# Tables built in place, outer products that ride, and wider VectorE operations in a fused S4D and channel-MLP kernel

## The chip, the cores and the metric

The kernel runs on one core of a Trainium2 chip. The metric is the time of one execution on the device in microseconds. Three runs of the kernel before gave a median of 1099.91 us (1099.19 to 1100.07). The engines are named as in the profile: PE (matrix multiplications), PEld (its weight loads), ACT (functions), DVE (vector operations), POOL and SP (here mostly queues that issue transfers).

## The reference

All arithmetic is in fp32. L is 2048 tokens, D 576 channels, N 128 states a channel, F 4608 hidden units. Cut to what matters:

```python
xn = layernorm(u)                                   # [L, D]
# S4D: a long convolution along the tokens, one kernel a channel
dt = exp(log_dt); A = -exp(log_A_real) + 1j * A_imag; C = (C_real + 1j * C_imag) * dt[:, None]
P = exp((A * dt[:, None])[:, :, None] * arange(L))  # [D, N, L]
K = 2 * einsum("dn,dnl->dl", C, P).real
s = irfft(rfft(xn.T, 2 * L) * rfft(K, 2 * L))[:, :L].T + xn * D_skip
# MLP, gated
y = layernorm(xn)
z = gelu(y @ w1 + b1) @ w2 + b2
out = u + s * silu(z)
```

## The kernel before

**The MLP is the backbone of PE's order.** The hidden units are taken in 12 groups of three times 128 (`NG`, `G`), and the tokens in two halves of two blocks of 512, which makes 48 passes (`slot`). A pass has 11 positions on PE: three layer-1 groups of 14 matmuls of 512 columns (`layer1`, L617), one for each 128 hidden units, and then eight stretches of layer 2 (`layer2`, L680, 288 columns), 72 matmuls. Each fp32 product is split into a high and a low part in fp32r, and three of the four partial products are taken. So for each layer-1 group ACT does the gelu into `h` (L653) and the high part `hh` (L656), and DVE the low part `hl` (L659). Layer 2 starts with the matmuls that need only the first two of the three hidden parts and then comes to the third. DVE adds layer 2's PSUM results to `acc` (L690). Weights come in by DMA into `raw` and are split in the same way (`split_raw`, L570 on ACT and L567 on DVE). In the 23rd and 24th pass the first half's output goes through a tanh for the gate (`gate_store`, L695), and y of the second half is turned and split (`y_turn`).

**The S4D part fills the gaps.** The length-2048 kernel of a channel is an outer product of two tables of powers, summed over the 128 states. `tables(b)` makes them for 16 channels (`SB`; 36 blocks): on DVE `phase` (L914, L917: the angle, 65 places a channel), on ACT `whole` (L920: the whole number of turns), on DVE `frac` (L923), on ACT `fold` (L926) and the two sines `sin` (L931 and L933), on DVE the magnitudes `mags` (L939) and `weigh` (L950 to L956), which multiplies the sines by the magnitudes into the tables `U` (32 places) and `v` (64 places). `kgen(b)` does the outer product on PE (`mm`, L995, 32 matmuls with 32 columns of weights and 64 of data) and copies it out of PSUM on ACT (`out`, L1000, into `kt`). `chunk(c)` then does the transforms of 96 channels (6 chunks): `x1` and `k1` (first stage of the transform for the data and the kernel, with a wide transpose on DVE behind it, L1107 and L1138), `s2` (second stage, L1160, then a copy `kk` on ACT, the products `pr` on DVE, L1175, and their sums, L1181 and L1182), `inverse` (L1202), `back` and `i1` (L1228). `in_parts` makes the high and low parts that `x1` and `k1` read.

**The order is written by a planner in the kernel itself.** The class `Order` holds lines of steps (`tl`, `sl`, `vl`: tables; `kl`: outer products; `c1` to `c4`: chunks) with durations for each engine, conditions (`need`, marks such as `("kg", b)` or `("wu", b, 1)`) and due times (`by`), and pins the resulting order on each engine. `pe_turns` lets S4D work onto PE between positions. An outer product that is ready when `x1`, `k1`, `s2` or `i1` goes can ride in front of it in the same PSUM tile (`ride`, `lead`); otherwise it goes alone when it has waited for `ALONE` us, or 3 us when the next table's sines are done and its due time (`DUE`) has passed. For a step of ACT that needs a table of functions, the planner adds 1.28 for each load; a step that needs none is only tested against the next due time:

```python
                    if st["tbl"]:
                        d += 1.28 * (1 + (st["tbl"] != self.tbl))
                    if b > horizon or b + d > soon.get(e, 1e9) + st["late"]:
                        continue
```

Of the kernel before, what the change touches and what calls it, by code (L numbers as in the profile page):

```python
# [210 lines left out]
def mixer_kernel(ctx, tc, u, log_a_real, a_imag, c_real, c_imag, log_dt, d_skip, w1, b1, w2, b2,  # L211
# [37 lines left out]

    idp = sb.tile([P, P], F32, name="idp")  # L250
    f1t = sb.tile([P, 2, 2, 64], F32, name="f1t")
# [110 lines left out]
    PT0 = 3 * D  # L362

    def table_memory():

        t = [sb.tile([P, 2, SB, NV], F32, name="w", bufs=2) for _ in range(2)]
        t = [x.rearrange("p k c t -> p (k c t)") for x in t + [sb.tile([P, 2, SB, 64], F32, name="v")]]
        return [t[k // 3][:, k % 3 * D:(k % 3 + 1) * D] for k in range(8)]

# [417 lines left out]
    def params():  # L787
# [7 lines left out]
        flat = lambda t: t.rearrange("p a b -> p (a b)")  # L795
        dt = sb.tile([P, 2, SB, 32], F32, name="U").rearrange("p a b c -> p (a b c)")[:, :D]
        PRM = [flat(sb.tile([P, 12, 64], F32, name="kt", bufs=2)) for _ in range(2)]
# [107 lines left out]
    def tables(b):  # L905
# [35 lines left out]

        def weigh(k, part):

            if k == 0 and part == 0:
                T["v"] = sb.tile([P, 2, SB, 64], F32, name="v")
                T["U"] = sb.tile([P, 2, SB, 32], F32, name="U")
                TAB[b] = (T["U"], T["v"])
            w, v, m = T["w"], T["v"], T["m"]
            if part == 0:
                nc.vector.tensor_mul(T["U"][:, k], w[:, k, :, 33:], m[:, :, 64:])  # L950
# [31 lines left out]
    def kgen(b):  # L982
# [16 lines left out]
        def out():  # L999
            nc.scalar.activation(KT[c, r // 48][:, k0:k0 + SB // 4, :].rearrange("p (h i) m -> p h (i m)", h=2),  # L1000
                                 Q[0], AF.Copy)
        need = [("kp", c - 1, r // 48)] if r % 48 == 0 and c else []
        return [step("PE", KG + 0.2, mm, need=need + [("wu", b, 1)], cv=1, mark=("kg", b)),
                step("ACT", act(256), out, cv=-1, mark=("kt", b))]
# [22 lines left out]
    def chunk(c):  # L1027
# [41 lines left out]
        def in_parts(which, i, get, m, need):  # L1069

            def high():
                a = sb.tile([P, 2, 4 * CH], F32R, name="pr").rearrange("p t c -> p (t c)")
                b = sb.tile([P, 2, 4 * CH], F32R, name="ys", bufs=2).rearrange("p t c -> p (t c)")
                PARTS2[which, i] = [t.rearrange("p (c b) -> p c b", b=m) for t in (a, b)]
                nc.scalar.activation(PARTS2[which, i][0], get(), AF.Copy)

            def low():
                a, b = PARTS2[which, i]
                nc.vector.tensor_sub(b, get(), a.bitcast(F32))

            n = 768 if which == "k" else 2000
            four.append(step("ACT", act(n), high, need=need))
            four.append(step("DVE", dve(n), low, mark=(which + "p", c, i)))
# [25 lines left out]

        def k1(i):  # L1110
# [6 lines left out]
            four.append(step("DVE", 0.2, skip, need=kt + ([] if c else [("pack", D // PK - 1), ("f2s", 7), "odd"] if i == 0 else [])))  # L1117
            in_parts("k", i, lambda: KT[c, i], 64, [("k1", c, i - 1) if i else ("x1", c, CH // 48 - 1)])

# [16 lines left out]
            add("PE", X1, mm, cv=2, mark=("k1", c, i), need=[("kp", c, i)] + ([("i1", c - 1)] if c and i == 0 else []))  # L1136
            for g in range(4):
                add("DVE", 0.65, lambda g=g: nc.vector.transpose(  # L1138
                    A2[:, :, 1, 48 * i + 12 * g:48 * i + 12 * g + 12].rearrange("p k d r -> p d k r"),
                    Q[g // 2 * 2][:, g % 2]),  # L1140
                    cv=-(g % 2))

        def s2(p):
# [5 lines left out]
            def mm():  # L1149
# [5 lines left out]
                for i in range(2):  # L1155
                    for ri in range(2):
                        for q in range(4):
                            for f in range(2):
                                r = slice(64 * f, 64 * f + 64)
                                nc.tensor.matmul(Q[i][32 * q:32 * q + 32, f, 2 * ri:2 * ri + 2],  # L1160
                                                 m[r, 4 * i + q, 32 * ri:32 * ri + 32],
                                                 A2[r, 4 * p + 2 * i + q // 2, :, :, q % 2], start=True, stop=True,
                                                 skip_group_check=True)
# [3 lines left out]
            def copy(i):  # L1167
                KK[i] = sb.tile([P, 2, 2, CH], F32, name="kk")
                nc.scalar.activation(KK[i], Q[i][:, :, 1::2], AF.Copy)

            def prod(i):

                PR[i] = sb.tile([P, 2, 4 * CH], F32, name="pr").rearrange("p t (a b d) -> p t a b d", a=2, b=2)
                for t in range(2):
                    nc.vector.tensor_mul(PR[i][:, t], bc(Q[i][:, t, 0::2], 2, 2), bc(KK[i][:, t], 1, 2))  # L1175

            def sums(i):
                if i == 0:
                    Y.append(ys_tile())
                x, y = PR[i], Y[0]  # L1180
                nc.vector.tensor_sub(y[:, i, 0], x[:, :, 0, 0], x[:, :, 1, 1])  # L1181
                nc.vector.tensor_add(y[:, i, 1], x[:, :, 0, 1], x[:, :, 1, 0])  # L1182
            for i in range(2):
                two.append(step("ACT", act(4 * CH), lambda i=i: copy(i), need=[("s2", c, p)]))
                two.append(step("DVE", 0.95, lambda i=i: prod(i), cv=-1))
                two.append(step("DVE", 0.63, lambda i=i: sums(i), mark=("sum", c, p) if i else None))
            if p % 2:
# [547 lines left out]
```

## Time and profile before

| | before |
|---|---|
| median of 3 runs | 1099.91 us (1099.19 to 1100.07) |
| the profiled execution | 1101.59 us |
| its span, first to last instruction | 1099.8 us |
| granted clock of PE | 0.999 |
| busy, PE and DVE and ACT | 1089.1, 918.8, 698.0 us |
| matmuls recorded | 11445 |
| instructions on DVE, on ACT | 1514, 1044 |
| loads of a function table on ACT | 84 |

The page of the profile gives the busy time of each engine, then the span in 40 slices, the DMA queues, the chain that ended last, and the costliest groups of instructions: the line in the kernel, engine, operation, the tiles written and read, the shapes, the count, busy us in all, mean ns of one, and the idle time before them with what ended it. A timeline row has the start in us from the span's start, the length in us, engine, line, tiles, shape and count; matmuls that follow each other in one group are merged into a row, and the recorded ends of matmuls overlap the next one's start, so distances are read from start to start. The same holds for DVE and ACT, whose operations overlap by some 0.1 us when they follow each other without a wait. An fp32 matmul is recorded twice, so the 32 of an outer product stand as 64.

### The profile page before, as it was taken

What the parts mean: (1) busy time and instruction counts of PE and PEld (TensorE: products, weight loads), DVE (VectorE), ACT (ScalarE), POOL (GpSimd) and SP (SyncE); (2) the same over time, 40 slices, a digit from 0 to 9 for tenths busy, and PEclk for the clock granted to TensorE, in tenths of its full rate; (3) what the DMA queues carried; (4) which work ended last, traced back from release to release, by engine and by line L of the source; (5) the groups of instructions that cost most, each with busy time, mean ns of one, the idle gap of its engine ahead of it and who ended that gap; (6) DMA issues with size and microseconds to landing.
All of it is one profiled execution on the core that took longest, in us unless ns stands there. A gap on an engine that the chain in (4) does not pass through costs nothing.

```text
span 1099.8 us, 27208 instructions
## 1 busy us (share of the span) xinstructions
PE 1089.1 (99%) x11445; PEld 953.2 (87%) x11445; DVE 918.8 (84%) x1514; ACT 698.0 (63%) x1044; POOL 184.0 (17%) x255
## 2 busy tenths in 40 slices
PE   8999999999999999999999999999999999999997
PEld 7889989889888888888898888888888888888897
DVE  7698678979998899999999998898998986766356
ACT  6485699867667675676865857566775754324233
POOL 4557211161110100001100000000100012110220
PEclk9999999999999999999999999999999999999999
DMA  8836656735434252355623315242333426453453
GB/s 222 242 131 169 219 173 197 215 71 130 152 115 152 53 112 57 100 128 149 154 51 95 96 56 126 39 143 59 94 89 78 145 66 178 117 178 107 128 148 94
DMA packets 139651, 138.23 MB, mean 126 GB/s; under 512 B 88952, under 2 KB 105016, under 8 KB 138952
## 3 DMA queue, kind: packets, MB, share of 16 engines
q1 hardware_dynamic: 124664, 85.49, 29.6%
q0 software_dynamic: 14384, 50.27, 14.8%
q8 instruction: 89, 1.46, 0.6%
q10 hardware_dynamic: 480, 0.74, 0.3%
q14 instruction: 34, 0.28, 0.1%
HBM read 102.17 MB, written 36.63 MB: 126 GB/s over the span
## 4 chain that ended last, share of the span: by engine, by line
PE 95%; DMA 2%; SPq 2%; DVE 1%; issue 0%; ACTq 0%; ACT 0%; DVEq 0%
PE mxb L680 21%; PE mxa L680 21%; PE mxa L617 20%; PE mxb L617 20%; PE cv L995 3%; PE cv L1160 3%; PE cv L1202 2%; PE cv L1228 2%; PE cv L1130 1%; PE cv L1099 1%; SPq L808 1%; DMA w<-in_A_u_dram 1%; DMA acc<-in_A_u_dram 0%; DVE st L407 0%; DMA h<-in_B_b_dram 0%
## 5 line engine op out<-in xcount | busy, mean ns | idle before, releaser
L659 DVE TENSOR_TENSOR hl<-h,hh 128x512 fp32r<-128x512 f32 x144 | 98.8, 689 | 89.0 <-ACT hh L656 88.3
L680 PE MATMUL mxb<-w2h,hl 128*128 128x288 f32 x576 | 170.2, 295 | 1.8 <-DVE hl L659 1.8
L680 PE MATMUL mxb<-w2h,hh 128*128 128x288 f32 x576 | 171.6, 298 | 0.0
L680 PE MATMUL mxa<-w2h,hh 128*128 128x288 f32 x573 | 170.8, 298 | 0.0
L680 PE MATMUL mxb<-w2l,hh 128*128 128x288 f32 x576 | 169.5, 294 | 0.0
L680 PE MATMUL mxa<-w2h,hl 128*128 128x288 f32 x573 | 169.2, 295 | 0.0
L680 PE MATMUL mxa<-w2l,hh 128*128 128x288 f32 x573 | 168.6, 294 | 0.0
L653 ACT ACTIVATE h<-mxa,b1t 128x512 f32<-128x512 f32 x73 | 50.2, 689 | 110.9 <-PE mxa L617 109.9
L680 PEld LDWEIGHTS mxa<-w2h,hh 128*128 128x128 f32 x573 | 107.6, 188 | 6.6 <-issue 3.5
L680 PEld LDWEIGHTS mxb<-w2h,hh 128*128 128x128 f32 x576 | 108.1, 188 | 5.7 <-issue 1.8
L680 PEld LDWEIGHTS mxb<-w2h,hl 128*128 128x128 f32 x576 | 108.1, 188 | 2.3 <-DVE hl L659 2.3
L680 PEld LDWEIGHTS mxb<-w2l,hh 128*128 128x128 f32 x576 | 108.1, 188 | 0.6
L680 PEld LDWEIGHTS mxa<-w2l,hh 128*128 128x128 f32 x573 | 107.6, 188 | 0.7
L680 PEld LDWEIGHTS mxa<-w2h,hl 128*128 128x128 f32 x573 | 107.5, 188 | 0.1
L896 POOL DMA_DIRECT2D par<-par_s x36 | 27.8, 773 | 462.9 <-DVE mg L939 458.4
L656 ACT ACTIVATE hh<-h 128x512 fp32r<-128x512 f32 x144 | 90.6, 630 | 3.6
L653 ACT ACTIVATE h<-mxb,b1t 128x512 f32<-128x512 f32 x71 | 48.9, 689 | 68.8 <-PE mxb L617 66.4
L690 DVE TENSOR_TENSOR acc<-mxa,acc 128x576 f32<-128x576 f32 x87 | 65.5, 752 | 31.2 <-PE mxa L680 30.9
L617 PE MATMUL mxa<-XH,w1h 128*128 128x512 f32 x284 | 79.1, 400 | 0.0
L690 DVE TENSOR_TENSOR acc<-mxb,acc 128x576 f32<-128x576 f32 x88 | 66.1, 752 | 15.2 <-PE mxb L680 14.8
L617 PE MATMUL mxb<-XH,w1h 128*128 128x512 f32 x280 | 77.7, 399 | 0.0
L617 PE MATMUL mxa<-XL,w1h 128*128 128x512 f32 x284 | 76.1, 390 | 0.0
(269 smaller groups left out, 2483.8 us busy)
## 6 DMA issues: line engine op xcount, KB each, us to landing
raw<-in_B_w_dram SPq DMA_DIRECT2D x72, 288.0 KB, 3.4
raw<-in_B_w_dram SPq DMA_DIRECT2D x96, 192.0 KB, 3.8
par_s<-A POOLq DMA_DIRECT2D x4, 2160.0 KB, 8.2
par<-par_s POOLq DMA_DIRECT2D x36, 240.0 KB, 3.4
f2t<-f2q SPq DMA_DIRECT2D x24, 256.0 KB, 3.4
g2t<-g2p SPq DMA_DIRECT2D x24, 256.0 KB, 4.1
bias<-XR SPq DMA_DIRECT2D x42, 128.0 KB, 3.7
raw<-in_B_w_dram SPq DMA_DIRECT2D x48, 96.0 KB, 3.9
```

Of the source, the lines that this page charges most:

```text
L617: nc.tensor.matmul(q, a, b, start=j == 0 and i not in BEGUN, stop=j == len(ops) - 1, skip_group_check=True)
L653: nc.scalar.activation(t, q, AF.Gelu_apprx_tanh, bias=b1t[:, k:k + 1], scale=1.0)
L656: LAST[0] = nc.scalar.activation(hh[:, i], t, AF.Copy)
L659: nc.vector.tensor_sub(hl[:, i], t, hh[:, i].bitcast(F32))
L680: nc.tensor.matmul(q[:, dh, :288], a[:, i, c], b[:, i, d], start=i == 0 and k == 0 and not alone, stop=i == G - 1 and k == 2)
L690: nc.vector.tensor_add(o, q[:, dh:dh + n, :288], b)
L808: nc.sync.dma_start(r[32 * g:32 * g + 32].rearrange("c (b n) -> c b n", n=32), dram(src[k], 32 * g, [[N, 32], [32 * N, D // 32], [1, 32]]))
L896: nc.gpsimd.dma_start(PAR[b].rearrange("p (g i) k -> p g (i k)", g=4), dram(par_s, (b // 3 * 48 + b % 3 * 4) * NPAR, [[D * NPAR, P], [12 * ...
L995: nc.tensor.matmul(q[32 * g:32 * g + 32, i // 2, i % 2 * 64:i % 2 * 64 + 64], U[:, ri, 4 * g + i, :], v[:, ri, 4 * g + i, :], start=ri == ...
L1160: nc.tensor.matmul(Q[i][32 * q:32 * q + 32, f, 2 * ri:2 * ri + 2], m[r, 4 * i + q, 32 * ri:32 * ri + 32], A2[r, 4 * p + 2 * i + q // 2, :, ...
L1202: nc.tensor.matmul(QI[q // 2][64 * f:64 * f + 64, q % 2, i], MAT["g2t", p + i // 2][r, i % 2, f, ri], YS[p + i // 2][0][r, i % 2, ri, f], ...
L1228: nc.tensor.matmul(Q[h][64 * y:64 * y + 64, t], g1t.rearrange("p a e -> p (a e)"), A2[:, k:k + 2, 1].rearrange("p i d r -> p i r d"), star ...
```

## The change

- The tables are built in place. One tile `w` of 97 places a channel (two of them in turn) holds the 65 angles and, in front, 32 places for the mirrored part. `weigh` has four steps rather than six: two over both sines at once (1024 elements), two of 512. They need the second sine; they no longer wait for `kg` of b-1. In exchange the first step of a table, `phase(0)`, waits for `("kg", b - 2)`, the outer product that read the tile, rather than for `("wu", b - 2, 1)`.
- An outer product goes alone early only when the next table is complete (`wu`, not only its sines), and otherwise after 20 us rather than 12. With `x1` it now rides behind the matmuls instead of in front.
- x's high and low parts are made from a contiguous copy `xt`, which ACT makes in a step of its own (`turn`).
- The transposes behind `x1` and `k1` take 768 elements rather than 384. In `s2` the results are interleaved (`ri::2`), `kk` gets a third, negated part by a second copy on ACT, and with it the products are one operation of 768 rather than two of 384, and the sums one of 384 rather than two of 192.
- The identity lies in the buffer of `f2t`, log dt in one of `ys`, and the early rows of x in two `w` tiles.

The diff, cut to its core:

```diff
-    idp = sb.tile([P, P], F32, name="idp")
+    idp = sb.tile([P, 4, P], F32, name="f2t")[:, 0]
...
+    def table_tile():
+        return sb.tile([P, 2, SB, 32 + NV], F32, name="w", bufs=2)
...
         def phase(k):
             if k == 0:
-                T["w"] = sb.tile([P, 2, SB, NV], F32, name="w", bufs=2)
+                T["v"] = table_tile()
+                T["w"] = T["v"][:, :, :, 32:]
...
+            if part == 0:
+                TAB[b] = (T["w"][:, :, :, 33:], T["v"][:, :, :, :64])
             w, v, m = T["w"], T["v"], T["m"]
             if part == 0:
-                nc.vector.tensor_mul(T["U"][:, k], w[:, k, :, 33:], m[:, :, 64:])
+                nc.vector.tensor_mul(v[:, :, :, :32], w[:, :, :, 32:0:-1], bc(m[:, :, :32], 1, 2))
             elif part == 1:
-                nc.vector.tensor_mul(v[:, k, :, :32], w[:, k, :, 32:0:-1], m[:, :, :32])
-            elif k == 0:
-                nc.vector.tensor_mul(v[:, k, :, 32:], w[:, k, :, :32], m[:, :, 32:64])
+                nc.vector.tensor_mul(w[:, :, :, 33:], w[:, :, :, 33:], bc(m[:, :, 64:], 1, 2))
+            elif part == 2:
+                nc.vector.tensor_mul(w[:, 0, :, :32], w[:, 0, :, :32], m[:, :, 32:64])
             else:
-                nc.vector.scalar_tensor_tensor(v[:, k, :, 32:], w[:, k, :, :32], -1.0, m[:, :, 32:64],
+                nc.vector.scalar_tensor_tensor(w[:, 1, :, :32], w[:, 1, :, :32], -1.0, m[:, :, 32:64],
                                                op0=OP.mult, op1=OP.mult)
...
-                 step("DVE", dve(SB * NV), f(phase, 0), need=[("wu", b - 2, 1)] if b > 1 else []),
+                 step("DVE", dve(SB * NV), f(phase, 0), need=[("kg", b - 2)] if b > 1 else []),
...
-                + [step("DVE", dve(n), f(weigh, k, part), need=[("sin", b, k)] + ([("kg", b - 1)] if b else []),
-                        mark=("wu", b, k) if part == 2 else None) for k in range(2) for part in range(3)])
+                + [step("DVE", dve((2, 2, 1, 1)[part] * n), f(weigh, part), need=[("sin", b, 1)],
+                        mark=("wu", b) if part == 3 else None) for part in range(4)])
...
+            def turn():
+                T["x"] = sb.tile([P, 24, m], F32, name="xt")
+                nc.scalar.activation(T["x"], get(), AF.Copy)
...
+            if which == "x":
+                four.append(step("ACT", act(2000), turn, need=need))
+            four.append(step("ACT", act(768), high, need=need if which == "k" else ()))
+            four.append(step("DVE", dve(768), low, mark=(which + "p", c, i)))
...
-                lead(q)
                 for n, (f, x) in enumerate(((0, a), (0, b), (1, a))):
...
+                lead(q)
             add("PE", X1, mm, cv=2, mark=("x1", c, i), need=[("xp", c, i)])
...
             for d0 in (0, 24):
-                for e in range(2):
-                    c0 = 48 * i + d0 + 12 * e
-                    add("DVE", 0.65, lambda d0=d0, e=e, c0=c0: nc.vector.transpose(
-                        A2[:, :, 0, c0:c0 + 12].rearrange("p k d r -> p d k r"), Q[d0][:, e]), cv=-e)
+                c0 = 48 * i + d0
+                add("DVE", 0.9, lambda d0=d0, c0=c0: nc.vector.transpose(
+                    A2[:, :, 0, c0:c0 + 24].rearrange("p k d r -> p d k r"), Q[d0]), cv=-1)
...
-                                nc.tensor.matmul(Q[i][32 * q:32 * q + 32, f, 2 * ri:2 * ri + 2],
+                                nc.tensor.matmul(Q[i][32 * q:32 * q + 32, f, ri::2],
...
-                KK[i] = sb.tile([P, 2, 2, CH], F32, name="kk")
-                nc.scalar.activation(KK[i], Q[i][:, :, 1::2], AF.Copy)
+                KK[i] = sb.tile([P, 2, 3, CH], F32, name="kk")
+                nc.scalar.activation(KK[i][:, :, :2], Q[i][:, :, :1:-1], AF.Copy)
+                nc.scalar.activation(KK[i][:, :, 2], Q[i][:, :, 3], AF.Copy, scale=-1.0)
...
-                for t in range(2):
-                    nc.vector.tensor_mul(PR[i][:, t], bc(Q[i][:, t, 0::2], 2, 2), bc(KK[i][:, t], 1, 2))
+                x, k = Q[i].rearrange("p t k d -> p t (k d)")[:, :, :2 * CH], KK[i].rearrange("p t k d -> p t (k d)")
+                k = bass.AP(tensor=k.tensor, offset=k.offset + CH, ap=[list(k.ap[0]), list(k.ap[1]), [-CH, 2], [1, 2 * CH]])
+                nc.vector.tensor_mul(PR[i], bc(x, 2, 2), k)
...
-                nc.vector.tensor_sub(y[:, i, 0], x[:, :, 0, 0], x[:, :, 1, 1])
-                nc.vector.tensor_add(y[:, i, 1], x[:, :, 0, 1], x[:, :, 1, 0])
+                nc.vector.tensor_add(y[:, i].rearrange("p a t d -> p t a d"), x[:, :, :, :CH], x[:, :, :, CH:])
...
-    ALONE, DUE = 12.0, (160.0, 950.0)
+    ALONE, DUE = 20.0, (160.0, 950.0)
...
-                    wait = ("sin", b + 1, 1) not in od.marks or od.t["PE"] < DUE[0] + b * (DUE[1] - DUE[0]) / NB
+                    wait = ("wu", b + 1) not in od.marks or od.t["PE"] < DUE[0] + b * (DUE[1] - DUE[0]) / NB
```

More of the change, by code (lines that the diff above doesn't have):

```diff
@@ L362, in mixer_kernel @@
     PT0 = 3 * D
+    def table_tile():
+        return sb.tile([P, 2, SB, 32 + NV], F32, name="w", bufs=2)
     def table_memory():
-        t = [sb.tile([P, 2, SB, NV], F32, name="w", bufs=2) for _ in range(2)]
-        t = [x.rearrange("p k c t -> p (k c t)") for x in t + [sb.tile([P, 2, SB, 64], F32, name="v")]]
-        return [t[k // 3][:, k % 3 * D:(k % 3 + 1) * D] for k in range(8)]
+        t = [table_tile().rearrange("p k c t -> p (k c t)") for _ in range(2)]
+        return [t[k // 4][:, k % 4 * D:(k % 4 + 1) * D] for k in range(8)]
     def x_load(b, queue=nc.sync, two=False):
@@ L795, in params @@
         flat = lambda t: t.rearrange("p a b -> p (a b)")
-        dt = sb.tile([P, 2, SB, 32], F32, name="U").rearrange("p a b c -> p (a b c)")[:, :D]
+        dt = ys_tile().rearrange("p i a b c -> p (i a b c)")[:, :D]
         PRM = [flat(sb.tile([P, 12, 64], F32, name="kt", bufs=2)) for _ in range(2)]
@@ L940, in mags, with weigh @@
                                  bc(PAR[b][:, :, e8:e8 + n], 3, 8), bc(PAR[b][:, :, e1:e1 + 8], 2, n))
[L942 to L947, printed above, removed]
+        def weigh(part):
+            if part == 0:
+                TAB[b] = (T["w"][:, :, :, 33:], T["v"][:, :, :, :64])
             w, v, m = T["w"], T["v"], T["m"]
             if part == 0:
-                nc.vector.tensor_mul(T["U"][:, k], w[:, k, :, 33:], m[:, :, 64:])
+                nc.vector.tensor_mul(v[:, :, :, :32], w[:, :, :, 32:0:-1], bc(m[:, :, :32], 1, 2))
             elif part == 1:
-                nc.vector.tensor_mul(v[:, k, :, :32], w[:, k, :, 32:0:-1], m[:, :, :32])
-            elif k == 0:
-                nc.vector.tensor_mul(v[:, k, :, 32:], w[:, k, :, :32], m[:, :, 32:64])
+                nc.vector.tensor_mul(w[:, :, :, 33:], w[:, :, :, 33:], bc(m[:, :, 64:], 1, 2))
+            elif part == 2:
+                nc.vector.tensor_mul(w[:, 0, :, :32], w[:, 0, :, :32], m[:, :, 32:64])
             else:
-                nc.vector.scalar_tensor_tensor(v[:, k, :, 32:], w[:, k, :, :32], -1.0, m[:, :, 32:64],
+                nc.vector.scalar_tensor_tensor(w[:, 1, :, :32], w[:, 1, :, :32], -1.0, m[:, :, 32:64],
                                                op0=OP.mult, op1=OP.mult)
@@ L1002, in kgen @@
         need = [("kp", c - 1, r // 48)] if r % 48 == 0 and c else []
-        return [step("PE", KG + 0.2, mm, need=need + [("wu", b, 1)], cv=1, mark=("kg", b)),
+        return [step("PE", KG + 0.2, mm, need=need + [("wu", b)], cv=1, mark=("kg", b)),
                 step("ACT", act(256), out, cv=-1, mark=("kt", b))]
@@ L1069, in in_parts, with source @@
         def in_parts(which, i, get, m, need):
+            T = {}
+            def turn():
+                T["x"] = sb.tile([P, 24, m], F32, name="xt")
+                nc.scalar.activation(T["x"], get(), AF.Copy)
+            def source():
+                return get() if which == "k" else T["x"].rearrange("p c b -> p (c b)")
             def high():
[L1072 to L1075, printed above, removed]
+                T["a"] = sb.tile([P, 2, 4 * CH], F32R, name="pr").rearrange("p t c -> p (t c)")
+                T["b"] = sb.tile([P, 2, 4 * CH], F32R, name="ys", bufs=2).rearrange("p t c -> p (t c)")
+                PARTS2[which, i] = [T[k].rearrange("p (c b) -> p c b", b=m) for k in "ab"]
+                nc.scalar.activation(T["a"], source(), AF.Copy)
             def low():
[L1078 to L1083, printed above, removed]
+                nc.vector.tensor_sub(T["b"], source(), T["a"].bitcast(F32))
+            if which == "x":
+                four.append(step("ACT", act(2000), turn, need=need))
+            four.append(step("ACT", act(768), high, need=need if which == "k" else ()))
+            four.append(step("DVE", dve(768), low, mark=(which + "p", c, i)))
         def x1(i):
@@ L1136, in k1 @@
             add("PE", X1, mm, cv=2, mark=("k1", c, i), need=[("kp", c, i)] + ([("i1", c - 1)] if c and i == 0 else []))
[L1137 to L1141, printed above, removed]
+            for g in (0, 2):
+                add("DVE", 0.9, lambda g=g: nc.vector.transpose(
+                    A2[:, :, 1, 48 * i + 12 * g:48 * i + 12 * g + 24].rearrange("p k d r -> p d k r"), Q[g]), cv=-1)
         def s2(p):
@@ L1180, in sums @@
                 x, y = PR[i], Y[0]
-                nc.vector.tensor_sub(y[:, i, 0], x[:, :, 0, 0], x[:, :, 1, 1])
-                nc.vector.tensor_add(y[:, i, 1], x[:, :, 0, 1], x[:, :, 1, 0])
+                nc.vector.tensor_add(y[:, i].rearrange("p a t d -> p t a d"), x[:, :, :, :CH], x[:, :, :, CH:])
             for i in range(2):
-                two.append(step("ACT", act(4 * CH), lambda i=i: copy(i), need=[("s2", c, p)]))
-                two.append(step("DVE", 0.95, lambda i=i: prod(i), cv=-1))
-                two.append(step("DVE", 0.63, lambda i=i: sums(i), mark=("sum", c, p) if i else None))
+                two.append(step("ACT", act(4 * CH) + act(2 * CH), lambda i=i: copy(i), need=[("s2", c, p)]))
+                two.append(step("DVE", dve(8 * CH), lambda i=i: prod(i), cv=-1))
+                two.append(step("DVE", dve(4 * CH), lambda i=i: sums(i), mark=("sum", c, p) if i else None))
             if p % 2:
```

4 lines of the change are left out of this document (2 added, 2 removed).

## The prediction

> **What bounds the kernel now.** I read the page first, then PE's timeline around the groups that the change moves, then ACT's and DVE's timeline where a pass turns from layer 1 to layer 2, and the groups by line and shape last.
>
> ```profile
> PE 1089.1 (99%) x11445; PEld 953.2 (87%) x11445; DVE 918.8 (84%) x1514; ACT 698.0 (63%) x1044; POOL 184.0 (17%) x255
> ...
> PE 95%; DMA 2%; SPq 2%; DVE 1%; issue 0%; ACTq 0%; ACT 0%; DVEq 0%
> ```
>
> PE is busy for 99% of the span and holds 95% of the chain that ended last. So the time is the length of PE's queue plus whatever makes PE wait. DVE at 84% and ACT at 63% are no bound as sums; they count only where PE arrives before their result. Waits of PE look like this in the timeline:
>
> ```profile
> 46.05 0.40 PE L680 MATMUL mxb<-w2h,hl 128*128 128x288 f32 x1 [1.19 <-DVE hl L659]
> 46.28 0.30 PE L680 MATMUL mxb<-w2h,hh 128*128 128x288 f32 x1
> ```
>
> Layer 2 waited 1.19 us for `hl`, and the next matmul came 0.23 after the late one where 0.13 is usual: a wait costs its length and 0.10 for the restart. After the first 50 us I find no further row of this kind: the order fits PE to within its margins. So two questions decide: how much shorter PE's queue gets, and whether the new order makes PE wait.
>
> **PE's queue.** An outer product (`kgen`, 32 matmuls in the program) alone between two layers:
>
> ```profile
> 610.42 0.39 PE L617 MATMUL mxb<-XR,w1s 128*128 128x512 f32 x1
> 610.74 1.10 PE L995 MATMUL cv<-v,U 128*32 128x64 f32 x64
> 611.77 0.96 PE L617 MATMUL mxa<-XH,w1h 128*128 128x512 f32 x3
> ```
>
> One that rides with `s2`, then `s2` without one, then the layer-1 matmuls in front of an `x1` by itself and behind it:
>
> ```profile
> 621.45 0.29 PE L680 MATMUL mxa<-w2h,hl 128*128 128x288 f32 x1
> 621.67 1.10 PE L995 MATMUL cv<-v,U 128*32 128x64 f32 x64
> 622.70 1.62 PE L1160 MATMUL cv<-A,f2t 64*32 64x192 f32 x64
> 624.25 0.40 PE L680 MATMUL mxb<-w2h,hh 128*128 128x288 f32 x1
> 624.49 0.29 PE L680 MATMUL mxb<-w2l,hh 128*128 128x288 f32 x1
> ...
> 632.08 0.39 PE L617 MATMUL mxb<-XR,w1s 128*128 128x512 f32 x1
> 632.39 1.59 PE L1160 MATMUL cv<-A,f2t 64*32 64x192 f32 x64
> 633.91 0.97 PE L617 MATMUL mxa<-XH,w1h 128*128 128x512 f32 x3
> ...
> 679.50 0.39 PE L617 MATMUL mxb<-XR,w1s 128*128 128x512 f32 x1
> ...
> 681.09 0.96 PE L617 MATMUL mxa<-XH,w1h 128*128 128x512 f32 x3
> ```
>
> A layer-1 matmul takes 0.226 from start to start, a layer-2 one 0.133 (rows below). Alone: 610.42 to 611.77 is 1.35, less 0.23 for the matmul in front, 1.12; and the first matmul behind such a group takes 0.24 instead of 0.13 (624.25 to 624.49), 0.11 more: 1.23. With `s2`: 621.45 to 624.25 less 0.13 is 2.67; `s2` by itself 632.08 to 633.91 less 0.23 is 1.60; the ride costs 1.07, and the 0.11 behind is paid once either way. `x1` by itself is 679.50 to 681.09 less 0.23, 1.36. So each product that stops going alone saves 0.16, or up to 0.20 if the host hides more.
>
> The order of the built programs gives the counts. Alone: 18 before, 7 after. With `s2` 12 and 14, with `k1` 5 and 5, with `i1` 0 and 4, with `x1` 1 and 6 (now behind its matmuls). Eleven fewer alone at 0.16 to 0.20 are 1.8 to 2.2; I take **-2.0 us**. Behind `x1` no row shows the price. If going from 64-row to 128-row weights costs a second switch of about 0.11, six of them give back 0.7; if the first step of `x1` no longer pays for one, they gain as much. I take the row of the ride. The strided destination of `s2` (`ri::2` in place of two neighbours) writes the same 192 columns in two runs of 96; no row shows it, and I take nothing, with 24 groups of 1.6 to bear it if not.
>
> **Where PE will wait.** The rows of ACT for one table (of sines) and the gelu behind it, and of the hand-over in one pass:
>
> ```profile
> 651.14 0.36 ACT L1000 ACTIVATE kt<-cv 128x256 f32<-128x256 f32 x1
> 651.40 1.06 ACT L933 ACTIVATE w<-w 128x1040 f32<-128x1040 f32 x1
> ...
> 722.10 1.28 ACT L931 ACT_TABLE_LOAD   x1
> 723.39 1.17 ACT L931 ACTIVATE w<-w,tv 128x1040 f32<-128x1040 f32 x1
> 724.46 0.47 ACT L1169 ACTIVATE kk<-cv 128x384 f32<-128x384 f32 x1
> 724.84 1.82 ACT L570 ACTIVATE w2h<-raw 128x576 fp32r<-128x576 f32 x3
> 726.56 1.06 ACT L933 ACTIVATE w<-w 128x1040 f32<-128x1040 f32 x1
> 727.64 1.28 ACT L653 ACT_TABLE_LOAD   x1
> 728.93 0.69 ACT L653 ACTIVATE h<-mxb,b1t 128x512 f32<-128x512 f32 x1
> ```
>
> ```profile
> 662.60 1.07 PE L617 MATMUL mxa<-XH,w1h 128*128 128x512 f32 x4
> 665.54 0.39 PE L617 MATMUL mxa<-XR,w1s 128*128 128x512 f32 x1
> 665.97 0.69 ACT L653 ACTIVATE h<-mxa,b1t 128x512 f32<-128x512 f32 x1 [0.45 <-PE mxa L617]
> 666.69 0.63 ACT L656 ACTIVATE hh<-h 128x512 fp32r<-128x512 f32 x1
> 666.89 0.40 PE L680 MATMUL mxb<-w2h,hh 128*128 128x288 f32 x1
> 667.35 0.69 DVE L659 TENSOR_TENSOR hl<-h,hh 128x512 fp32r<-128x512 f32 x1 [2.25 <-ACT hh L656]
> 668.59 0.29 PE L680 MATMUL mxa<-w2h,hh 128*128 128x288 f32 x1
> ```
>
> A layer-1 group: 662.60 to 665.54 is 13 matmuls, 0.226 each; 14 and the slow first one are 3.28. In layer 2, 666.89 to 668.59 is 12 matmuls with the slow first, 0.133 each. Layer 2 begins with 18 matmuls that need only the first two groups of hidden units, 2.39; then two that need the third `hh`; then, at 2.66, the third `hl`.
>
> In the order before, no table load stands between the gelus of one pass in any of the 48 passes. In the changed order it does in three, the 16th, 22nd and 30th: between the second `hh` and the third gelu stand a load, the cosine, `kt`, and in two of the three also the two `kk` copies and the whole-number step of the next table, then the load back. The cause is in the diff: the first table step now waits for `kg` of b-2, which rides, so that `kt`, `kk` and that step come ready together behind the same group, after the planner had let the cosine in; its test for those short steps counts no load back.
>
> Worked from the last matmul of the second group at 0. PE: 0.23, the ride with `s2` 2.67, the third group 3.28: layer 2 begins at 6.18 and wants the third `hl` at 8.84. ACT: gelu at 0.43 (665.54 to 665.97), `hh` at 1.14 to 1.77, load, cosine at 3.08 (1.29 from load to it), `kt` at 4.15 (1.07), `kk` at 4.41 (0.26), its negated third at 4.79 (0.38), the whole-number step at 5.00, the load back at 6.08 (1.08, as 726.56 to 727.64), gelu at 7.37, `hh` at 8.09 (0.72), `hl` at 8.75 (0.66) to 9.44. That is 0.60 late, with 0.05 until PE starts and two restarts 0.85. (The negated third, 192 elements, has no row; it lies between 0 and the 0.38 of 384 elements, and 0.2 by their slope.) In the 22nd pass DVE's fractional step of 1.23 stands right ahead of `hl`: 0.2 more, 1.05. In the 30th the copies and the whole-number step are missing, 1.57 less on ACT, but a fold of 1.07 stands ahead of the second gelu, and `x1` with a product, 2.43, brings PE 0.24 earlier: 0.34 late, and 0.6 with the restarts. Together **+2.5**, between 0 (if PE comes later than I think) and 4.
>
> [...]
>
> One more load. The gates' tanh (L695, 16 of them) had the gelu set at hand in the order before. In the changed order a table of sines ends just ahead of one, the program then loads a set that has tanh and not gelu, and the gelu of the 25th pass needs another load. That is 1.28 on ACT where y's parts, w2's parts, gate and x's new copy stand back to back, and DVE is filled with the same things. Between 0 and 1.4; I take **+1.0**, nearer to the whole, as neither queue has idle time there by these rows' lengths.
>
> **DVE's wider operations.**
>
> ```profile
> L950 DVE TENSOR_TENSOR U<-w,mg 128x512 f32<-128x512 f32 x72 | 49.2, 683 | 3.7 <-PE cv L995 2.3 <-ACT w L931 0.7
> L939 DVE TENSOR_TENSOR mg<-par 128x1024 f32<-128x1024 f32 x36 | 44.0, 1222 | 0.7
> ```
>
> Twice 512 elements is 1.37, once 1024 is 1.22: 0.15 less for a pair. So the 72 pairs of weights and 48 each of products, transposes and sums that are joined save some 30 us. DVE is not the bound, so this is worth 0 in itself. But a long operation is not broken off: an `hl` that comes ready just behind one waits up to 0.54 longer than behind 512 elements. The usual margin is small: the third `hl` can end 0.4 before PE wants it (0.43 + 0.72 + 0.66 + 0.69 from the group's last matmul, against 2.66 + 0.23). I take **+0.5** for a few such places, between -0.2 and 3. ACT gets 48 negated copies and 12 turns of x, some 25 us in its idle 37%; SP and POOL move no transfer that PE waits for. The buffers that move (the identity into `f2t`'s, log dt into `ys`'s, x's rows into the two `w` tiles) leave the order up to the first table as it was: 0, covered by the 150 us before it.
>
> **The sum**: -2.0 + 2.5 + 1.0 + 0.5 = +2.0. The profiled execution took 1101.59 with a span of 1099.8; the median of the runs is 1099.91, and the difference is added to that: **1101.9 us**. A measurement of this kernel can tell about 0.2% (2.2 us) from no change, so this lies just inside.
>
> **Rivals.** (1) The waits do not come: PE reaches the third `hl` later than worked out, as it did in all passes before. Then only PE's queue counts, 1097.9. For it speaks that no wait shows after 50 us; against it, that no pass before had two loads in that place. 7%. (2) The wide forms cost more than their size: products that read PSUM and step backwards, tables with a row of 97. With each 0.1 longer, the stretches in which DVE runs without a gap push `hl` and the accumulations past PE in some ten more places at 0.2 to 0.4: 1104 to 1106. It decides from about 0.05 an operation on, as the margin is 0.4 and eight of them fit between two groups. For it: none of these forms has a row. 25%. (3) The products ride on paper only: behind `x1` and ahead of `i1` PE switches as often as before, ten times 0.2 back, 1103.9, or half of it. 4%. [...]
>
> **Numbers.** Forecast 62%, with a range of its own of 1100.5 to 1103.3; of that 37% lie within 0.2% and 25% above. Rival 1: 6% faster, 1% within. Rival 2: 25% slower. Rival 3: 2% and 2%. Rival 4: 2% slower. Faster 0.06, same 0.40, slower 0.54. The range takes the forecast's own and most of rival 2: 1100.0 to 1105.0.
>
> **What would show it.** Right: 7 groups of `kg` alone, PE's rows at 1.1 for a product behind `x1`; `mxb<-w2h,hl` with a wait on `hl` or `hh` in three passes, each behind two table loads between second and third gelu; a load at the gate's tanh and an `acc` that comes late behind it. Wrong: no waits on `hl` after 50 us (rival 1), or waits in many passes without a load near (rival 2).

## The result, and the profile after

The changed kernel takes 1102.94 us in the median of ten runs (1101.74 to 1103.59), the kernel before in ten runs on the same chip 1099.69 (1099.18 to 1100.32). The ratio is 1.0029 with a 95% interval of 1.0019 to 1.0038: slower by 3.2 us, give or take 1. The forecast was 1101.9, slower by 2.0, in a range of 1100.0 to 1105.0.

Busy times and the chain that ended last, from the page of the changed kernel:

```profile
PE 1090.1 (99%) x11445; PEld 954.5 (87%) x11445; DVE 892.8 (81%) x1298; ACT 725.7 (66%) x1109; POOL 184.1 (17%) x255
...
PE 87%; DVE 4%; ACT 3%; DMA 2%; SPq 2%; issue 1%; POOL 0%; ACTq 0%; DVEq 0%; POOLq 0%
```

DVE lost 26 us of work and 216 instructions, ACT gained 28. Neither sum matters. What matters is that PE's share of the chain fell from 95% to 87%, and that DVE and ACT, 1% and 0% before, now hold 7%. The waits of PE from 60 to 1085 us say where; the columns are the tile and line that waited, what it waited for, us in all, times, and the longest:

```profile
PE mxa L682 <- DVE acc L692: 1.0, 1, 1.0
PE mxa L682 <- ACT h L655: 0.5, 2, 0.2
PE mxa L682 <- issue: 0.4, 1, 0.4
PE mxa L682 <- DVE hl L661: 0.4, 1, 0.4
PE mxb L682 <- DVE hl L661: 0.2, 1, 0.2
```

The same view of the kernel before is empty. It counts idle time from a matmul's recorded end, which lies 0.16 beyond the next regular start, and it leaves the restart out. So I add the spacing from start to start beyond the regular 0.226 and 0.132, from 60 to 1085 us, and do the same for the groups between the layers (from the matmul in front to the second one behind; some groups of both kernels have a pair of 64-row matmuls ahead, whose price is taken off):

| | before | after |
|---|---|---|
| products alone | 18 at 1.23 | 7 at 1.23 |
| `s2` with one, without | 12 at 2.78, 12 at 1.72 | 14 at 2.76, 10 at 1.74 |
| `x1` with one, without | 1 at 2.59, 11 at 1.47 | 6 at 2.48, 6 at 1.44 |
| `i1` with one, without | 0, 6 at 3.05 | 4 at 4.09, 2 at 3.06 |
| all groups between layers | 160.55 us | 158.25 us |
| stops beyond the regular spacing | 1.28 us, of it 14 times 0.09 where such a pair begins | 6.64 us, of it 15 times 0.09 where such a pair begins |

PE's queue is 2.3 shorter and its stops are 5.4 longer: +3.1, against +3.2 in the runs.

The two profiled executions differ by only 1.2 (1101.59 and 1102.84). The rest lies in the first 50 us: in the profile of before, the 400th matmul of the layers starts at 81.60 us, after the stops around 46 us that the prediction shows; in the eleven other profiles here it starts between 78.7 and 79.8. That execution was slow at the start by chance, 1.9 above its own median, and adding the difference to the median was the right base.

### The profile page after: what moved, and what is told of

Its sections match the earlier page's. It is cut to its first block, busy times and chain, and to the rows that moved or that the text cites. A ratio compares the mean times of both kernels' runs of the same rounds, so it can differ in the third digit from the quotient of the medians.

```text
span 1101.0 us, 27023 instructions
## 1 busy us (share of the span) xinstructions
PE 1090.1 (99%) x11445; PEld 954.5 (87%) x11445; DVE 892.8 (81%) x1298; ACT 725.7 (66%) x1109; POOL 184.1 (17%) x255
## 4 chain that ended last, share of the span: by engine, by line
PE 87%; DVE 4%; ACT 3%; DMA 2%; SPq 2%; issue 1%; POOL 0%; ACTq 0%; DVEq 0%; POOLq 0%
PE mxb L682 19%; PE mxa L682 19%; PE mxb L619 18%; PE mxa L619 18%; PE cv L1167 3%; PE cv L996 3%; PE cv L1210 2%; PE cv L1139 1%; PE cv L1108 1%; PE cv L1236 1%; SPq L810 1%; DMA row<-g_s 1%; DMA w<-in_A_u_dram 1%; SPq L385 1%; ACT h L655 0%
```

## The experiments

The theory is that of the prediction: the queue gives 2.3, table loads between the second and third gelu of three passes take 2.5, and a load at the gates' tanh 1.2. The rivals put the loss on DVE's wide operations, or on an order without slack in which any wait taken away comes back. Each kernel's ratio is against the kernel before in the same rounds (medians there 1099.05 to 1099.27); the changed kernel stands at 1.0029, from the rounds of the result, and was not run again beside them.

**The load at the gates.** Rows of ACT, DVE and PE in the changed kernel:

```profile
531.45 1.28 ACT L697 ACT_TABLE_LOAD   x1
...
539.45 1.28 ACT L655 ACT_TABLE_LOAD   x1
...
541.80 0.46 DVE L708 SCALAR_TENSOR_TENSOR acc<-h,acc 128x288 f32<-128x288 f32 x1 [1.15 <-ACT h L697]
...
552.11 0.75 DVE L692 TENSOR_TENSOR acc<-mxa,bias 128x576 f32<-128x576 f32 x1
...
551.62 0.29 PE L682 MATMUL mxb<-w2h,hl 128*128 128x288 f32 x1
552.91 0.40 PE L682 MATMUL mxa<-w2h,hh 128*128 128x288 f32 x1 [1.00 <-DVE acc L692]
```

The second load at 539.45 makes a gate's tanh late, DVE stands idle for 1.15, is full from there on, and reaches `acc` that much later.

```diff
-            T.append(tanh_half(z))
+            od.tbl == "gelu" or nc.scalar.activation(small[:, 5:6], epst[:, 0:1], AF.Gelu_apprx_tanh)
+            T.append(tanh_half(z))
```

> The changed kernel with one gelu of a single element put ahead of the one gate tanh that finds the table of sines loaded; the load ahead of it then brings a set that has both functions, and nothing else moves. Theory (the extra table load makes the accumulations of the 25th pass late): the second load 8 us later is gone, the wait of 1.16 on acc at 551.6 and its restart of 0.10 go with it, 1102.9 - 1.25 = 1101.7. Rival (DVE is simply full there, with 1.85 of transposes and 1.2 of the next table ahead of acc): one load fewer on ACT changes nothing for DVE, the wait stays over 0.8, 1102.5 to 1103.

1100.85 us, ratio 1.0015 (1.0006 to 1.0024). ACT and PE of this run:

```profile
530.55 1.28 ACT L705 ACT_TABLE_LOAD   x1
531.85 0.20 ACT L705 ACTIVATE tv<-tv 128x1 f32<-128x1 f32 x1
...
550.75 0.29 PE L682 MATMUL mxb<-w2h,hl 128*128 128x288 f32 x1
551.10 0.40 PE L682 MATMUL mxa<-w2h,hh 128*128 128x288 f32 x1
```

One load serves gelu and tanh (the tanh at 531.96 and the next gelu at 538.54 follow without another), the load ahead of that gelu is gone, and the distance at the stop falls from 1.29 to 0.35. By the ratios the gain is 0.14%, 1.5 us, where 1.25 was expected. The theory stands; a stop of 0.32, restart included, is left for DVE alone.

**The sines between the gelus.** The 22nd pass of the changed kernel, ACT, then DVE, then PE:

```profile
475.73 1.18 ACT L934 ACTIVATE w<-w,tv 128x1040 f32<-128x1040 f32 x1
476.81 0.36 ACT L1001 ACTIVATE kt<-cv 128x256 f32<-128x256 f32 x1
477.08 0.47 ACT L1176 ACTIVATE kk<-cv 128x384 f32<-128x384 f32 x1
477.45 0.32 ACT L1177 ACTIVATE kk<-cv 128x192 f32<-128x192 f32 x1
477.66 1.09 ACT L923 ACTIVATE w<-w 128x1040 int32<-128x1040 f32 x1
478.77 1.28 ACT L655 ACT_TABLE_LOAD   x1
480.06 0.69 ACT L655 ACTIVATE h<-mxa,b1t 128x512 f32<-128x512 f32 x1
...
481.61 0.68 DVE L661 TENSOR_TENSOR hl<-h,hh 128x512 fp32r<-128x512 f32 x1
...
480.80 0.40 PE L682 MATMUL mxa<-w2h,hh 128*128 128x288 f32 x1 [0.24 <-ACT h L655]
481.83 0.29 PE L682 MATMUL mxb<-w2l,hh 128*128 128x288 f32 x1
482.35 0.40 PE L682 MATMUL mxb<-w2h,hl 128*128 128x288 f32 x1 [0.22 <-DVE hl L661]
```

This is the sequence that was forecast, step by step, with two stops and two restarts. In the experiment the first sine of these three tables is an absolute value of the same shape:

```diff
-                nc.scalar.activation(w, w, AF.Sin, bias=halfpi[:, 0:1], scale=-TWO_PI)
+                nc.scalar.activation(w, w, AF.Abs if b in (9, 16, 24) else AF.Sin, bias=halfpi[:, 0:1], scale=-TWO_PI)
```

> The changed kernel with the first sine of three tables (those whose sine stands between the second hh and the third gelu of the 16th, 22nd and 30th pass) computed as an absolute value instead, an operation of the same shape that needs no table; all else in the same order. Theory (the two table loads around it make the third hh and hl late): the loads go, 2.57 on ACT, and with them the waits of 0.82, 0.99 and 0.69 (restarts in): 1102.9 - 2.5 = 1100.4, and the wait on acc at 551.6 stays at 1.2. Rival (hl is late because DVE's wider operations stand ahead of it, as the fractional step of 1.20 does in the 22nd pass): the 22nd pass keeps over 0.3, and the total gains under 1.5: 1101.4 to 1102.9.

1099.53 us, ratio 1.0005 (0.9996 to 1.0014): 0.24% less than the changed kernel, 2.6 us. The same pass in its trace, ACT and PE:

```profile
477.43 0.69 ACT L655 ACTIVATE h<-mxa,b1t 128x512 f32<-128x512 f32 x1 [0.88 <-PE mxa L619]
...
479.74 0.29 PE L682 MATMUL mxb<-w2l,hh 128*128 128x288 f32 x1
479.89 0.40 PE L682 MATMUL mxb<-w2h,hl 128*128 128x288 f32 x1
```

The gelu now waits for PE and not PE for it; of 0.99 at this place 0.10 is left, at the other two nothing, and the stop at the gates stays (1150 ns of extra spacing). So it was the loads, and not the operation of 1.2 that stands ahead of `hl` on DVE in this pass.

**Both together.** The two edits above in one kernel.

> Both edits together: three first sines computed as absolute values, and one gelu ahead of the gate's tanh. Theory (the two causes are independent, and PE's queue is 2.3 shorter than before): 1102.9 - 2.5 - 1.25 = 1099.2, 0.5 below the kernel before, with waits of PE of 1.4 after 60 us where the kernel before has none. Rival (PE has no slack left anywhere, so a wait taken away comes back at the next hand-over): the sum gains less than 2.5, 1100.5 or more.

1098.87 us, ratio 0.9998 (0.9989 to 1.0006), 3.4 us below the changed kernel by the ratios where 3.75 was expected. Its view of PE's waits is empty again; the stops by spacing add up to 2.4 beside 1.3 before. The two causes add within the intervals, and nothing came back elsewhere. With a part of its sines left out, this is what the change would have been worth in this order without its waits: no difference that can be told.

**DVE's width.** Each widened operation of the changed kernel issued as two narrow ones, all else in the same order, for example:

```diff
-                nc.vector.tensor_mul(w[:, :, :, 33:], w[:, :, :, 33:], bc(m[:, :, 64:], 1, 2))
+                [nc.vector.tensor_mul(w[:, k, :, 33:], w[:, k, :, 33:], m[:, :, 64:]) for k in range(2)]
```

> The changed kernel in its own order, but each of DVE's widened operations (two table products, the products and sums behind s2, the transposes behind x1 and k1) issued as the two narrow ones of before; 216 more instructions and some 26 us more busy time on DVE. Theory (DVE is no bound as a sum, yet hl and acc stand in its queue, so width is worth what it takes away in the few dense stretches of this order): slower, waits on hl and acc in some four more places at 0.2 to 0.5, 1104 to 1106. Rival 1 (the long operations themselves make hl late, so the narrow ones let it in earlier): faster than the changed kernel, 1101.5 to 1102.5. Rival 2 (DVE has idle time everywhere it matters): 1102.9 within 0.4.

1104.96 us, ratio 1.0052 (1.0040 to 1.0065), 0.23% slower than the wide form. Its waits of PE from 60 us on:

```profile
PE mxa L682 <- DVE acc L692: 1.5, 2, 1.2
PE mxa L682 <- ACT h L655: 0.8, 3, 0.4
PE mxb L682 <- DVE hl L661: 0.7, 2, 0.4
```

So the wide operations do not block `hl`. With the narrow ones DVE's dense stretches are longer: the waits that were there grow (at 458 us from 0.16 to 0.51 without the restart, at the gates' `acc` from 1.15 to 1.31), and new ones of 0.3 to 0.5 come at 576, 719 and 860 us. The groups of the wide forms in the changed kernel (count, busy us, mean ns):

```profile
L1184 DVE TENSOR_TENSOR pr<-cv,kk 128x768 f32<-128x768 f32 x48 | 45.6, 951 | 9.4 <-ACT kk L1177 9.3
L951 DVE TENSOR_TENSOR w<-w,mg 128x1024 f32<-128x1024 f32 x36 | 43.8, 1216 | 1.6 <-ACT w L936 1.6
L1190 DVE TENSOR_TENSOR ys<-pr 128x384 f32<-128x384 f32 x48 | 26.6, 555 | 1.2
L1116 DVE STREAM_TRANSPOSE A<-cv 128x768 f32<-128x768 f32 x24 | 22.4, 964 | 1.2 <-PE cv L1108 1.2
```

These are the durations that size alone gives, by the 683 ns for 512 elements and 1222 for 1024 of before: on their line 768 take 952 and 384 take 548. Yet the narrow kernel keeps DVE busy for 903.6 us and the wide one for 892.8: 216 instructions fewer are worth 10.8, 0.05 each, not the 0.15 that the durations say.

**The place of the product in x1's group.** `lead(q)` again ahead of the matmuls:

```diff
+                lead(q)
                 for n, (f, x) in enumerate(((0, a), (0, b), (1, a))):
...
-                lead(q)
```

> The changed kernel with the outer product again ahead of x1's matmuls in the six groups where it rides with x1; all else in the same order. Theory (behind x1 the product saves a switch of tile shape on PE: 2.37 for the pair in the changed kernel, 2.48 in the one group of before that had it in front): six times 0.11 longer, 1102.9 + 0.6 = 1103.5, less what PE's later arrival takes off the waits, 0.2. Rival (a guest's place in its group is worth nothing, and the 0.11 came from what stood ahead of that one group): 1102.9 within 0.2, the six groups at 2.37.

1102.76 us, ratio 1.0031 (1.0020 to 1.0042): no difference. The first of the six groups, PE, in the changed kernel and then in this run:

```profile
236.76 0.39 PE L619 MATMUL mxb<-XR,w1s 128*128 128x512 f32 x1
...
238.33 1.10 PE L996 MATMUL cv<-w 128*32 128x64 f32 x64
239.36 0.97 PE L619 MATMUL mxa<-XH,w1h 128*128 128x512 f32 x3
```

```profile
235.75 0.39 PE L619 MATMUL mxb<-XR,w1s 128*128 128x512 f32 x1
236.07 1.10 PE L996 MATMUL cv<-w 128*32 128x64 f32 x64
...
238.36 1.20 PE L619 MATMUL mxa<-XH,w1h 128*128 128x512 f32 x4
```

From the matmul in front to the first behind it is 2.60 and 2.61; over the six groups the median with the restart is 2.480 behind and 2.494 in front. My 0.11 was a miss: it came from one group of before that had other work ahead of it, a pair of 64-row matmuls. In the one group of the six that has such a pair (at 393 us) the place does count: 2.71 behind, where `x1`'s 64-row matmuls follow the pair directly, and 2.91 in front, where the product's 128-row ones come between. One group of 0.20 is too little to show in the time.

**The going-alone rule.**

```diff
-    ALONE, DUE = 20.0, (160.0, 950.0)
+    ALONE, DUE = 12.0, (160.0, 950.0)
...
-                    wait = ("wu", b + 1) not in od.marks or od.t["PE"] < DUE[0] + b * (DUE[1] - DUE[0]) / NB
+                    wait = ("sin", b + 1, 1) not in od.marks or od.t["PE"] < DUE[0] + b * (DUE[1] - DUE[0]) / NB
```

> The changed kernel with the two numbers of the going-alone rule as before: a product may wait only while the second sine of the next table is missing (instead of its last weighing), and for 12 us instead of 20. The order after the first tables becomes another one: 14 or 15 products alone instead of 7, fewer with s2, x1 and i1. Theory (a product alone costs PE 0.16 to 0.20 more than one that rides; the table steps that wait for the product two tables earlier are what brings sines between the gelus of a pass, whatever the rule): PE's queue 1.3 to 1.6 longer than in the changed kernel, and table loads again between second and third gelu in some passes, with waits of 1 to 3 in all where the changed kernel has 5.2 with its jitter: 1101 to 1103.5. Rival (the rule is what puts the sines there, by tying products and tables together): no load between the gelus of any pass, waits under 0.5 and only the queue's length counts: 1099 to 1100.

1100.48 us, ratio 1.0010 (1.0001 to 1.0019), between the theory's range and the rival's. Fourteen products go alone, and the groups between layers add up to 159.6, 1.4 more than after. Stops are 3.7 instead of 6.6. One of them, of 0.65 in the 20th pass, has the same form as before:

```profile
428.38 1.28 ACT L934 ACT_TABLE_LOAD   x1
429.67 1.19 ACT L934 ACTIVATE w<-w,tv 128x1040 f32<-128x1040 f32 x1
430.76 0.38 ACT L1001 ACTIVATE kt<-cv 128x256 f32<-128x256 f32 x1
431.02 0.49 ACT L1176 ACTIVATE kk<-cv 128x384 f32<-128x384 f32 x1
431.39 0.34 ACT L1177 ACTIVATE kk<-cv 128x192 f32<-128x192 f32 x1
431.75 1.28 ACT L655 ACT_TABLE_LOAD   x1
433.05 0.69 ACT L655 ACTIVATE h<-mxa,b1t 128x512 f32<-128x512 f32 x1
```

So the loads between gelus don't hang on the rule: the order of this kernel has them in the 20th, 22nd and 33rd pass. That the first table step's new wait for the product brings them, as the prediction says, is argued and was not tested by itself. Beside the new condition the built order is the same for 12 and 20, so `ALONE` has no part in the changed kernel; beside the old one it is not (14 products alone with 12, 13 with 20). So the condition accounts for six of the seven products that go alone here and not in the changed kernel, and the order that came with it cost more than the 1.4 it saves.

**A planner that leaves room.** Nothing left out; a sine must have 2.0 us to spare, and the gelu ahead of tanh as above:

```diff
-                        d += 1.28 * (1 + (st["tbl"] != self.tbl))
+                        d += 1.28 * (1 + (st["tbl"] != self.tbl)) + (2.0 if st["tbl"] == "sin" else 0.0)
```

> The changed kernel, with nothing left out, where a sine is let in only if 2.0 us more than itself and its loads are free before the next due step of ACT (the room that kt, kk and the whole-number step take when they come ready behind it), and with the gelu of one element ahead of a gate tanh that finds sines loaded. The order becomes another one: nine products alone. Theory: no load stands between the gelus of a pass, no late acc at the gates; the queue is 0.3 to 1.3 longer than in the changed kernel (two more alone, fewer of the paired 64-row matmuls that go ahead of a group): 1099 to 1100. Rival (an order without these waits has others, since DVE and ACT are fuller than before): 1101 or more.

1104.17 us (1102.83 to 1106.23), ratio 1.0046 (1.0034 to 1.0059): a clear miss. No load stands between gelus, but PE waits elsewhere:

```profile
PE cv L1108 <- DVE ys L1088: 0.7, 1, 0.7
PE mxa L682 <- DVE acc L692: 0.5, 1, 0.5
PE cv L1108 <- ACT kt L1001: 0.3, 1, 0.3
PE cv L1108 <- ACT pr L1085: 0.3, 1, 0.3
```

In this order two `x1` follow each other closely, x's rows land late (ACT stood idle for 4.22 until they were there, at 964.00), and the new copy `xt` of 2.11 on ACT, the high part and the low part come after them: 2.1 at one `x1`, 0.8 at an `acc` behind another. The granted clock was lower as well, 0.996 to 0.998 in its five runs and 0.998 to 1.000 in those of the other experiments. The profiled execution, at 0.998, took 1102.83 us, and the four at 0.996 and 0.997 took 1104.13 to 1106.23. So a part of the 0.46% may go with the clock; how much, and why the clock was lower, is open.

**And other spacing for x1.** The room of the kernel above, without the extra gelu, which this order does not need, and

```diff
-    EDGE = 0.2, 0.6
+    EDGE = 0.2, 0.68
```

> The changed kernel, with nothing left out, where a sine needs 2.0 us more room as in the run before, and the next x1 may come between the layers of a pass from 0.68 of its mean distance on instead of 0.6. Eight products alone, 14 with s2, five with x1, seven with k1, three with i1, no load between the gelus of any pass. Theory (queue 2.0 to 2.4 shorter than before and no wait over 0.2 after 60 us): 1097.0 to 1097.6, 0.2% faster than the kernel before. Rival (waits come back in places that no load marks): 1099 or more.

1096.70 us (1096.10 to 1097.59), ratio 0.9977 (0.9968 to 0.9987): faster than both kernels, by 2.5 us than the one before, and a little under the range given. Its chain is PE's again, and one wait is left after 60 us, 0.3 where none over 0.2 was expected:

```profile
PE 94%; DVE 2%; SPq 1%; DMA 1%; issue 1%; ACT 0%; POOL 0%; DVEq 0%; POOLq 0%
```

```profile
PE mxa L682 <- DVE acc L692: 0.3, 1, 0.3
```

**The same two numbers without the change**, in the kernel before:

> The kernel before with the two numbers of the planner that made the changed kernel faster (a sine needs 2.0 us more room; the next x1 from 0.68 of its mean distance on). 19 products alone instead of 18, nine with s2, and no load between the gelus of a pass. Theory (the two numbers only spare the new order its waits; what is faster is the shorter queue that the change allows): no gain, 1099.0 to 1101. Rival (the numbers alone are what is better, and the change has no part in it): 1098 or less.

1101.68 us, ratio 1.0022 (1.0013 to 1.0031). Slower, by more than expected: one layer-1 group waits for its gelu there, with 1.1 of extra spacing at 823 us, and an `acc` comes 0.3 late at 526 us. The numbers are not better in themselves; they fit the changed kernel's work. What each of the two does alone for the changed kernel stays open: the room was run only with the extra gelu (above, slower), the spacing alone was not run.

**Narrow operations in the faster version.**

> The faster version (the changed kernel with the two numbers) in its own order, but each of DVE's widened operations issued as the two narrow ones of before. Theory (in an order without loads between the gelus DVE's width is worth little: hl and acc have room): 0.3 to 1.0 slower than with the wide ones, waits of 0.1 to 0.4 in two or three places, 1097.0 to 1097.9. Rival (width is worth the 2.0 that it was in the changed kernel's order, wherever it stands): 1098.5 or more.

1097.03 us, ratio 0.9978 (0.9969 to 0.9987), the same as with wide ones (0.9977), where 0.3 to 1.0 us slower was expected. Where next to nothing is late, DVE's width is worth nothing that can be measured.

## Why the prediction was right

**PE's queue: -2.0 forecast, -2.3 measured.** The counts (7 alone, 14, 5, 4 and 6 riding) came out. The price was mis-sized: a ride costs 1.02 to 1.04 with each of the four hosts of the changed kernel, the 1.07 that I took stands only in the rows of `s2` before, and each product that stops going alone saves 0.20 instead of 0.16 to 0.20. Behind `x1` the price is the same (1.04), and rival 3 is out. The strided destination of `s2` costs 0.02 alone and gains 0.02 with a guest: the 0 holds.

**Three passes: +2.5 forecast, 2.50 measured,** as 0.82, 0.99 and 0.69 for the forecast 0.85, 1.05 and 0.60, each with the order of operations that was worked out. The experiment without the loads took away 2.6 by the ratios. The negated third of `kk`, without a row then, starts 0.21 ahead of the next operation; 0.2 was taken. Rival 1 (no waits) is out. No run shows a load that costs more than its row, to which the chances give 2% as rival 4: the load of 1.28 at 478.77 is followed by the gelu at 480.06, and the six loads that went took 2.6 with them.

**The gate: +1.0 forecast, 1.26 measured,** and 1.5 by the ratios of the run without the second load. I had reasoned "nearer to the whole", and it was 1.15 of DVE's idle time passed on in full, as no queue had slack.

**DVE: +0.5 forecast for long operations in front of `hl`; this step failed in its mechanism.** No late `hl` or `acc` of the changed kernel comes directly behind a widened operation (at the gates two wide transposes stand two operations ahead of the late `acc`, which came later still with narrow ones), and the narrow ones were slower in its order and equal in the faster one. Rival 2, with 25% the largest, falls with it. That a long operation is not broken off holds: in both profiles no operation of DVE starts more than 0.19 before the end of the one ahead of it. The working had two faults. The "30 us" that the pairs save were durations; back to back these operations overlap (in the kernel before three of 0.68 start at 729.22, 729.82 and 730.42, so by 0.08), and the width saved 10.8 of busy time, while half of the 26 by which DVE's work fell, near the 30 only by luck, came from the contiguous `xt` (L1079 took 2056 ns for x's parts before, L1088 takes 953 now). And I took the length of an operation for the delay of the next without a place where it happens. One instruction fewer was worth 0.05 us of busy time here, in the mean of the 216, of which 120 read SBUF alone and 96 PSUM.

**What stood there instead** is 1.6 us of other stops, 1.4 of it in three: 0.27 for an `acc` that comes late behind the magnitudes (458.6 us, a form that didn't change), 0.62 for an `hl` at 932.7 us behind two operations on `row` whose data landed 8.3 us after the issue, where the prediction saw no transfer that PE waits for, and 0.49 behind an inverse. Between kernels of the same order the second comes and goes and the third varies. They make most of the step from the forecast +2.0 to +3.1; -2.3 + 2.5 + 1.26 + 1.6 is 3.1. So the two large waits were foreseen with their mechanism, and it is luck that the +0.5 stood, with the right sign, where stops of another kind came.

## What to carry to other kernels

When work becomes ready at another moment, look at what the scheduler will put in front of it: the gain of 2.3 us on the busiest engine's queue was real, and two function-table loads in three places outweighed it. The rows suggest that a due-time test must count the load back to the table that the next due step needs, for steps that need no table too; that test itself was not run. What was run is plain room ahead of the next due step: with the old spacing of the work around it (and the extra gelu) it made an order that was 0.5% slower, and with another spacing it turned 0.3% slower into 0.2% faster. Take a saving per instruction from the distance between starts in a dense stretch, not from durations: here the durations said 0.15 and the busy time fell by 0.05.

## What the runs showed of the hardware

One stop of PE has no releaser. In or right behind the same inverse, PE lost 0.19 to 0.81 us in all six kernels that share the changed order; none of their eleven other inverses did, and none of the twelve of before. Rows of the changed kernel:

```profile
739.62 1.83 PE L1210 MATMUL cv<-ys,g2t 32*64 32x96 f32 x128
741.87 0.40 PE L682 MATMUL mxa<-w2h,hh 128*128 128x288 f32 x1 [0.42 <-issue]
```

Its inputs had been done for over 2 us. An inverse has 128 recorded matmuls and as many weight loads in 1.8 us. In the 4 us from 738 on, the instruction queue moved one packet, of 0.02 MB, which took 1.4 us. That instructions came late is a guess; no run tested it, and it does not say why the other inverses run through. The runs with three sines left out and with the product in front of `x1` have one more stop without a releaser each, 0.38 at 868 us and 0.59 at 870 us.

With a table of 97 places a channel instead of 65, ACT's operations on 1040 elements are slightly longer though the count of elements is the same: the cosine from 1166 to 1185 ns, the sine from 1060 to 1086, the whole-number step from 1069 to 1084.
